# A recurrent attention step: the second V cast placed ahead of the second half's exponentials, and the second half's memory-query sums placed behind all of V's matmul groups

## Chip, cores and metric

The kernel runs on one core of a Trainium2 chip. The metric is the device time of one execution in microseconds (us). The kernel before takes 770.77 us, the median of three runs (770.53 to 771.61).

## What is computed

The output mixes two branches with a gate per token: `g * a + (1 - g) * b`. Branch `b` is a layer norm followed by a two-layer MLP with a gelu. Branch `a` is what most of the time goes to: attention over 64 segments of 32 tokens, in order, because each segment takes eight memory rows from the one before it.

```python
mem = mem0
for s in range(n_seg):                       # 64 segments, strictly one after another
    xs = x[:, s * seg_len:(s + 1) * seg_len, :]
    h = jnp.concatenate([mem, xs], axis=1)   # 8 memory rows + 32 tokens
    q, k, v = (einsum('btd,dhe->bhte', h, W) for W in (Wq, Wk, Wv))   # 32 heads of 128
    scores = where(mask, q @ k^T * scale, -1e9)
    p = softmax(scores)
    o = einsum('bhqk,bhke->bhqe', p, v)
    o = einsum('bhte,hed->btd', o, Wo)
    mem = o[:, :M, :]                        # rows of the 8 memory queries: the next segment's memory
    outs.append(o[:, M:, :])
return concatenate(outs, axis=1)
```

## The kernel before

A first stage computes the MLP branch and loads the attention weights. Then a loop of 64 steps (line 678 and on), one per segment, does the attention. Everything in a step hangs on the memory rows that the step before delivered, so the steps can't overlap, except for work that doesn't need the memory: the last eight tokens of each segment are projected for four segments at a time, and these "fill" units are handed out by `run(n)` at places in the step where TensorE would wait. The order of instructions on each engine is written out by hand (a manual schedule); each engine works through its own list in that order, and semaphores make it wait for others. The code's order is therefore the whole schedule.

What a step does, in the order of TensorE (PE in the profile), with the lines that the prediction uses:

1. Four projections for Q and K, sixteen matmuls each (`qk_unit`, L122), each cast by ScalarE (ACT, L127) and transposed by VectorE (DVE, L131).
2. `scores(s, 0)`: scores of heads 0 to 15 into PSUM bank `SbF` (L259, L263), then ScalarE's exponential over them into `E` (L713).
3. V of heads 0 to 15 into bank `X1`: four groups of four matmuls (`v_unit`, L141), one group for each 128 rows of the contraction (`kc`). The four matmuls of a group stand in four column strips of the array. Then the first group of V for heads 16 to 31 into bank `X2`.
4. `xsums(E, 0)` (L616) and `msum(0)` (L270, L273): small matmuls with a matrix of ones that add up the exponentials, of the token queries and of the memory queries. `mnorm(0)` on VectorE takes the reciprocal of the memory queries' sums (L709) and multiplies them onto their exponentials (L710).
5. `scores(s, 1)`: scores of heads 16 to 31 into bank `W`. On ScalarE: `exps(1, 0)` for the memory queries (64 columns, L702), the second cast of V's first half, `v_cast(0, 1)` (L719), and `exps(1, 1)` for the token queries (160 columns, L702).
6. Two more groups of V into `X2` (`kc` 1 and 2), then `msum(1)` with `mnorm(1)`, then V's last group (`kc` 3). ScalarE casts `X2` in two halves, `v_cast(1, 0)` and `v_cast(1, 1)` (L719).
7. Two fill units, `xsums(E, 1)` (L616), and `av`: exponentials times V into the four banks `U`, first heads 0 to 15 (sixteen L283, four L288), then heads 16 to 31 (the same again). The second sixteen need the product of `mnorm(1)` and the casts of `X2`: the first eight of them `v_cast(1, 0)`, the last eight `v_cast(1, 1)`.
8. ScalarE copies the memory queries' part out of `U` (L746), TensorE projects with Wo (L153), and eight small matmuls and three casts (L659, L661) turn the result into the next step's memory rows.

`mnorm(1)` is more tied up than it looks: its reciprocal reads the sums in `U[1]`, and writes into a spare part of bank `W`, the bank from which `exps(1, 1)` reads its scores. So it waits for `msum(1)` on TensorE and for `exps(1, 1)` on ScalarE, whichever is later.

The last step (s = 63) has no `msum` and no `mnorm`, and ends in a tail of its own.

Of the kernel before, what the change touches and what calls it, by code (L numbers as in the profile page):

```python
# [27 lines left out]
def kernel(ctx, tc, A_x, A_mem0, A_Wq, A_Wk, A_Wv, A_Wo, A_seg_len, B_x, B_w1, B_b1, B_w2, B_b2, gate_w, out):  # L28
# [9 lines left out]
    KC = Dm // P  # L38
# [55 lines left out]
    def load_xT(T):  # L94
        xT = ew.tile([P, KC, P], BF16, tag="xT", bufs=3, name="xT")
        nc.sync.dma_start_transpose(out=xT[:], in_=x2[T * P:(T + 1) * P, :])
        xTs[T] = xT
# [9 lines left out]
    X2 = lps.tile([P, 512], FP32)  # L107
# [11 lines left out]
    def qk_unit(bk, G, t, hf, kc):  # L119
        h0, h1 = HF[hf]  # L120
        for j in range(4):
            nc.tensor.matmul(bk[32 * j:32 * j + 32, :], lhsT=G[:, kc, :], rhs=W5[t][:, kc, h0:h1, j, :],  # L122
                             start=(kc == 0), stop=(kc == KC - 1), tile_position=(0, 32 * j))

    def qk_cast(bk):
        Tb = ew.tile([P, 8, 32, 2], BF16, tag="Tb", bufs=3, name="Tb")
        nc.scalar.copy(out=Tb[:], in_=bk.rearrange("p (a b e) -> p a e b", a=8, b=2))  # L127
        return Tb

    def qk_tr(Tb, dst, hf, c0=0):  # L130
        nc.vector.transpose(out=dst[:, 8 * hf:8 * hf + 8, c0:c0 + 32, :].rearrange("p a r b -> p a (r b)").bitcast(FP32),  # L131
                            in_=Tb[:].rearrange("p a e b -> p (a e b)").bitcast(FP32))
# [6 lines left out]
    def v_unit(bk, G, vb, kc):  # L139
        for j in range(4):  # L140
            nc.tensor.matmul(bk[32 * j:32 * j + 32, :], lhsT=G[:, kc, :], rhs=Wv5[:, kc, 4 * vb:4 * vb + 4, j, :],  # L141
                             start=(kc == 0), stop=(kc == KC - 1), tile_position=(0, 32 * j))
# [18 lines left out]
    def flush(q, n=1):  # L161
        for _ in range(min(n, len(q))):
            q.pop(0)()
# [17 lines left out]
    def vp_load(T, si):  # L181
        nc.sync.dma_start(VP[T % 2][:, si].rearrange("p v e -> p (v e)"), VLs[T][si:P:SPT].rearrange("p a v e -> p a (v e)"))
# [20 lines left out]
    def c_load(T):  # L203
        c = cw.tile([P, Dm], BF16, tag="c", name="c")
        nc.sync.dma_start(c[:], c_dr[T * P:(T + 1) * P, :])
        cs[T] = c
# [30 lines left out]
    def prep_h(s):  # L237
        T, si = divmod(s, SPT)
        nc.gpsimd.tensor_copy(out=hT[s % 3][:, :, 0:RIDE], in_=xTs[T][:, :, seg * si:seg * si + RIDE])
# [14 lines left out]
    def scores(s, i2):  # L254
        T, si = divmod(s, SPT)
        for i in range(4 * i2, 4 * i2 + 4):
            for j in range(4):
                h = 4 * i + j
                nc.tensor.matmul(Sb[i2][32 * j:32 * j + 32, i - 4 * i2, M:M + 40], lhsT=KT[:, h // 2, :, h % 2], rhs=QT[:, h // 2, :, h % 2],  # L259
                                 start=False, stop=True, skip_group_check=True, tile_position=(0, 32 * j))  # L260
        for j in range(4):
            a0 = 8 * i2 + j // 2
            nc.tensor.matmul(Sb[i2][32 * j:32 * j + 32].rearrange("p i (a b) -> p i a b", b=8)[:, :, 0:7:6, :],  # L263
                             lhsT=KL[T % 2][:, si, j // 2, i2].rearrange("p l a b -> p (l a) b")[:, :, j % 2],
                             rhs=QT[:, a0:a0 + 7:2, :, j % 2].rearrange("p a (x q) -> p a x q", q=8)[:, :, 0:5:4, :],
                             start=False, stop=True, skip_group_check=True, tile_position=(0, 32 * j))
# [323 lines left out]
    def side(T, si):  # L590
        gens = []
        if si == 2:
            if T >= 1:
                gens.append(wo_left(T - 1, X1))
        elif T + 1 < NT:
            gens = [[left_qk(T + 1, 0, 0, X1), left_qk(T + 1, 1, 0, X2)], [left_qk(T + 1, 0, 1, X1), left_qk(T + 1, 1, 1, X2)], [],
                    [left_v(T + 1, 0, X1), left_v(T + 1, 1, X2)]][si]
        return chain(*gens)
# [39 lines left out]
    def x_norm(s):  # L638
        T, si = divmod(s, SPT)
        XR, Rb = XRs.pop(s), Rbs.pop(s)[:].rearrange("p (c q) (h j) -> p h j c q", c=4, h=2)  # L640
        for out, o, a, b in ((UT[(s + 1) % 2], M, LEFT, 32), (UL[T % 2], LEFT * si, 0, LEFT)):
            for h in range(2):
                nc.gpsimd.tensor_tensor(out=out[:, :, 4 * h:4 * h + 4, o:o + b - a], in0=XR[:, :, 4 * h:4 * h + 4, a:b], in1=Rb[:, h, :, :, a:b], op=ALU.mult)  # L643
# [21 lines left out]
    for s in range(nseg):  # L665
        T, si = divmod(s, SPT)
        last = s == nseg - 1
        hc, hn = hT[s % 3], hT[(s + 1) % 3]
        W1, W2, W3 = WS[si]
        fill = side(T, si)  # L670
        if s + 1 < nseg:
            prep_h(s + 1)
        if s >= 1:
            x_norm(s - 1)
        if si == 0 and T >= 2:
            c_load(T - 2)
        if si < 3:
            vp_load(T, si + 1)
        if last:
            c_load(T - 1)  # L680
            c_load(T)
        if si == 0 and T + 2 < NT:
            load_xT(T + 2)
        for n, (t, hf) in enumerate(((0, 0), (1, 0), (0, 1), (1, 1))):
            bk = U[n]
            for kc in range(KC):
                qk_unit(bk, hc, t, hf, kc)
            if n == 0:
                flush(act_q, 9)
                flush(dve_q, 9)  # L690
            qk_tr(qk_cast(bk[:]), (QT, KT)[t], hf, LEFT * (1 - t))
            if n == 0:
                mask_put(1)
        V = cw.tile([P, NG, Dh], BF16, tag="V", name="V")
        E = cw.tile([P, NG, EW], BF16, tag="E", name="E")
        R = cw.tile([P, NG * 40], FP32, tag="R", name="R")
        Rs[s] = R
        xsum = SbF[:, 0:32 * NG].rearrange("p (i q) -> p i q", q=32)

        def exps(i2, x):  # L700
            c = slice(0, 40) if x else slice(40, EW)
            nc.scalar.activation(out=E[:, 4 * i2:4 * i2 + 4, c], in_=Sb[i2][:, :, c], func=ACTF.Exp, scale=scale)  # L702

        def msum(i2):
            sums(U[i2][:, 320:352].rearrange("p (i q) -> p i q", q=8), E[:, 4 * i2:4 * i2 + 4, :], 40, 48, 8, True)

        def mnorm(i2):
            r, e = RP[i2], E[:, 4 * i2:4 * i2 + 4, 40:56].rearrange("p i (a q) -> p i a q", q=8)
            nc.vector.reciprocal(out=r, in_=U[i2][:, 320:352])  # L709
            nc.vector.tensor_tensor(out=e, in0=e, in1=r.rearrange("p (i q) -> p i q", q=8).unsqueeze(2).to_broadcast([P, 4, 2, 8]), op=ALU.mult)  # L710

        scores(s, 0)
        nc.scalar.activation(out=E[:, 0:4, :], in_=Sb[0], func=ACTF.Exp, scale=scale)  # L713
        for kc in range(KC):
            v_unit(X1, hc, 0, kc)

        def v_cast(vb, h):
            i0 = 4 * vb + 2 * h
            nc.scalar.copy(out=V[:, i0:i0 + 2, :].rearrange("p i e -> p (i e)"), in_=(X1, X2)[vb][:, 256 * h:256 * h + 256])  # L719

        v_cast(0, 0)
        v_unit(X2, hc, 1, 0)
        if not last:
            xsums(E, 0)
            msum(0)
            mnorm(0)
        scores(s, 1)
        exps(1, 0)
        v_cast(0, 1)
        exps(1, 1)  # L730
        for kc in range(1, KC - 1):
            v_unit(X2, hc, 1, kc)
        if not last:
            msum(1)
            mnorm(1)
        v_unit(X2, hc, 1, KC - 1)
        for h in range(2):
            v_cast(1, h)
        if last:
            break  # L740
        run(W1)
        xsums(E, 1)
        recip_x(s)
        av(s, V, E)
        for j in (0, 2, 1, 3):
            nc.scalar.copy(out=UT[s % 2][:, j, :, 0:M], in_=U[j][:, 0:NG * 40].rearrange("p (i q) -> p i q", q=40)[:, :, 32:40])  # L746
        x_raw(s)
        run(W2)
        prep_q(s + 1)
        w = wo_pass(UT[s % 2], (0, P, 2 * P, Dm))  # L750
        if s >= 1:
            ws[s - 1] = w
        run(W3)
        for _ in extra(T, si):
            pass
        new_mem(w, hn, 0)
        run(1)
        new_mem(w, hn, 1)
        run(1)
        new_mem(w, hn, 2)  # L760
        for _ in fill:
            pass
        if si == 3 and T + 2 < NT:
            left_x(T + 2)
        flush(dve_q, 9)
        nc.vector.tensor_tensor(out=rmin[:, 0:RW], in0=rmin[:, 0:RW], in1=R[:, 0:RW], op=ALU.min)
        flush(act_q, 9)
# [174 lines left out]
```

## Time and profile before

| | |
|---|---|
| median of the runs | 770.77 us (770.53 to 771.61) |
| the profiled execution's own time: its span, first to last instruction | 768.4 us |
| what the median has beyond that span | 2.4 us |
| mean granted TensorE clock | 0.996 of full speed |
| busy: PE, ACT, DVE, POOL | 753.4, 540.0, 396.1, 278.2 us |
| bytes moved by DMA | 70.58 MB, 92 GB/s on average |

A row of the timeline gives the start in us, the duration in us, the engine, the line, the operation, what it writes and reads, the shape, and how many such instructions in a row were put together (x8). A duration of a merged row runs from the first start to the last end. PE is matmuls, PEld the loading of their stationary operand, which runs beside PE. In brackets stands how long the engine had been idle and what let it go on.

Busy time of PE has to be read with care: a matmul's row covers its way through the array, some 0.17 us for the smallest, and the next ones start long before it ends. A PE that waits 0.1 us for a semaphore still looks nearly busy. Waits are better read from the starts of two neighbouring rows.

### The profile page before, as it was taken

What the parts mean: (1) busy time and instruction counts of PE and PEld (TensorE: products, weight loads), DVE (VectorE), ACT (ScalarE), POOL (GpSimd) and SP (SyncE); (2) the same over time, 40 slices, a digit from 0 to 9 for tenths busy, and PEclk for the clock granted to TensorE, in tenths of its full rate; (3) what the DMA queues carried; (4) which work ended last, traced back from release to release, by engine and by line L of the source; (5) the groups of instructions that cost most, each with busy time, mean ns of one, the idle gap of its engine ahead of it and who ended that gap; (6) DMA issues with size and microseconds to landing.
All of it is one profiled execution on the core that took longest, in us unless ns stands there. A gap on an engine that the chain in (4) does not pass through costs nothing.

```text
span 768.4 us, 43822 instructions
## 1 busy us (share of the span) xinstructions
PE 753.4 (98%) x19186; PEld 412.2 (54%) x19186; DVE 396.1 (52%) x1428; ACT 540.0 (70%) x1631; POOL 278.2 (36%) x522
## 2 busy tenths in 40 slices
PE   7999999999999999999999999999999999999996
PEld 5666554555555555555555555555555555555553
DVE  5776355445445454545554554545454555444444
ACT  4666676777777777777777777777777777777763
POOL 4111033433344443334434334443424443343341
PEclk9999999999999999999999999999999999999999
DMA  6779422223222222212131322122222213122221
GB/s 196 274 233 400 153 58 63 76 63 87 65 59 66 79 72 73 80 53 74 58 89 62 90 63 79 45 80 73 80 72 59 76 49 89 62 83 64 72 67 38
DMA packets 53319, 70.58 MB, mean 92 GB/s; under 512 B 21306, under 2 KB 43043, under 8 KB 51587
## 3 DMA queue, kind: packets, MB, share of 16 engines
q1 hardware_dynamic: 51394, 64.84, 26.8%
q8 instruction: 152, 2.49, 1.4%
q0 software_dynamic: 784, 1.97, 0.8%
q10 hardware_dynamic: 944, 0.92, 0.3%
q14 instruction: 45, 0.36, 0.2%
HBM read 56.96 MB, written 4.45 MB: 80 GB/s over the span
## 4 chain that ended last, share of the span: by engine, by line
PE 96%; DMA 1%; DVE 1%; ACT 1%; issue 0%; SPq 0%; POOL 0%; DVEq 0%; ACTq 0%
PE U L122 30%; PE X L141 18%; PE W L153 15%; PE X L122 7%; PE U L468 4%; PE U L283 4%; PE X L153 4%; PE W L462 2%; PE SbF L462 2%; PE U L270 1%; PE W L259 1%; DMA w_sb<-in_B_w_dram 1%; PE U L659 1%; PE SbF L259 1%; PE SbF L616 1%; PE U L288 1%
## 5 line engine op out<-in xcount | busy, mean ns | idle before, releaser
L643 POOL TENSOR_TENSOR UT<-XR,Rb 128x384 bf16<-128x384 bf16 x126 | 140.3, 1136 | 301.7 <-DMA Rb<-r_dr 220.5
L127 ACT CAST Tb<-U 128x512 bf16<-128x512 f32 x258 | 151.2, 586 | 78.4 <-PE U L122 78.1
L122 PEld LDWEIGHTS <-hT 128*32 128x32 bf16 x4096 | 104.5, 96 | 103.9 <-DVE hT L661 8.6
L141 PE MATMUL X<-Wv_sb,hT 128*32 128x512 bf16 x2048 | 143.8, 378 | 0.0
L122 PE MATMUL U<-Wq_sb,hT 128*32 128x512 bf16 x2048 | 136.1, 381 | 0.3 <-DVE hT L661 0.2
L122 PE MATMUL U<-Wk_sb,hT 128*32 128x512 bf16 x2048 | 132.7, 379 | 0.0
L153 PE MATMUL W<-Wo_sb,UT 128*32 128x512 bf16 x2080 | 124.6, 380 | 1.2 <-POOL racc L635 1.2
L661 DVE CAST hT<-U 128x8 bf16<-128x8 f32 x126 | 20.9, 167 | 172.8 <-PE U L659 163.6
L719 ACT CAST V<-X 128x256 bf16<-128x256 f32 x256 | 88.7, 372 | 14.5 <-PE X L141 0.8
L131 DVE STREAM_TRANSPOSE QT<-Tb 128x256 f32<-128x256 f32 x128 | 57.0, 446 | 76.5 <-ACT Tb L127 76.5
L153 PEld LDWEIGHTS <-UT 128*32 128x32 bf16 x2080 | 57.8, 96 | 56.5 <-issue 13.1
L650 ACT CAST w<-W 128x128 bf16<-128x128 f32 (+1 forms) x192 | 46.0, 311 | 48.2 <-PE W L153 48.2
L622 ACT CAST XR<-U 128x256 bf16<-128x256 f32 x252 | 78.4, 434 | 0.0
L131 DVE STREAM_TRANSPOSE KT<-Tb 128x256 f32<-128x256 f32 x128 | 57.0, 445 | 28.0 <-ACT Tb L127 23.5
L643 POOL TENSOR_TENSOR UL<-XR,Rb 128x128 bf16<-128x128 bf16 x126 | 60.3, 502 | 0.0
L141 PEld LDWEIGHTS <-hT 128*32 128x32 bf16 x2048 | 46.4, 94 | 21.0
L635 POOL TENSOR_TENSOR racc<-racc,R 128x72 f32<-128x72 f32 x63 | 21.3, 338 | 93.4 <-PE U L288 84.1
L468 PE MATMUL U<-w_sb,hTm 128*128 128x512 bf16 (+1 forms) x176 | 52.4, 381 | 0.0
L746 ACT CAST UT<-U 128x64 bf16<-128x64 f32 x252 | 35.4, 226 | 22.9 <-PE U L288 22.8
L462 PEld LDWEIGHTS <-w_sb 128*128 128x128 bf16 (+1 forms) x352 | 34.5, 102 | 20.1 <-issue 1.3
L702 ACT ACTIVATE E<-W 128x64 bf16<-128x64 f32 (+1 forms) x128 | 35.0, 273 | 11.3 <-PE W L263 11.3
L659 PEld LDWEIGHTS <-w 128*32 128x32 bf16 x1008 | 22.8, 93 | 37.2 <-ACT w L650 29.3
(159 smaller groups left out, 1204.7 us busy)
## 6 DMA issues: line engine op xcount, KB each, us to landing
Rb<-r_dr SPq DMA_DIRECT2D x63, 512.0 KB, 3.8
Wv_sb<-in_A_Wv_dram SPq DMA_DIRECT2D x4, 1024.0 KB, 6.3
Wq_sb<-in_A_Wq_dram SPq DMA_DIRECT2D x4, 1024.0 KB, 7.1
Wk_sb<-in_A_Wk_dram SPq DMA_DIRECT2D x4, 1024.0 KB, 9.4
Wo_sb<-in_A_Wo_dram SPq DMA_DIRECT2D x4, 1024.0 KB, 15.0
VP<-VL SPq DMA_DIRECT2D x64, 64.0 KB, 3.5
c<-c_dr SPq DMA_DIRECT2D x16, 128.0 KB, 3.6
xt<-in_A_x_dram SPq DMA_DIRECT2D x15, 128.0 KB, 3.1
```

Of the source, the lines that this page charges most:

```text
L122: nc.tensor.matmul(bk[32 * j:32 * j + 32, :], lhsT=G[:, kc, :], rhs=W5[t][:, kc, h0:h1, j, :], start=(kc == 0), stop=(kc == KC - 1), tile_ ...
L127: nc.scalar.copy(out=Tb[:], in_=bk.rearrange("p (a b e) -> p a e b", a=8, b=2))
L131: nc.vector.transpose(out=dst[:, 8 * hf:8 * hf + 8, c0:c0 + 32, :].rearrange("p a r b -> p a (r b)").bitcast(FP32), in_=Tb[:].rearrange("p ...
L141: nc.tensor.matmul(bk[32 * j:32 * j + 32, :], lhsT=G[:, kc, :], rhs=Wv5[:, kc, 4 * vb:4 * vb + 4, j, :], start=(kc == 0), stop=(kc == KC - ...
L153: nc.tensor.matmul(bk[32 * c:32 * c + 32, :], lhsT=U_[:, j, i, :], rhs=Wo_sb[:, 4 * i + j, :], start=(n == 0), stop=(n == NW - 1), tile_po ...
L462: nc.tensor.matmul(hp[:rows, 0:TB * P], lhsT=w1_sb[:, kc, fc * P:fc * P + rows], rhs=yTs[blk][:, kc, :], start=(kc == 0), stop=(kc == KC - 1))
L468: nc.tensor.matmul(bp(blk, tt)[:], lhsT=hTm[blk % 2][:rows, fc, tt * P:(tt + 1) * P], rhs=w2_sb[:rows, fc, :], start=(fc == 0), stop=(fc = ...
L622: nc.scalar.copy(out=XR[:, j], in_=U[j][:, 0:NG * 40].rearrange("p (i q) -> p i q", q=40)[:, :, 0:32])
L643: nc.gpsimd.tensor_tensor(out=out[:, :, 4 * h:4 * h + 4, o:o + b - a], in0=XR[:, :, 4 * h:4 * h + 4, a:b], in1=Rb[:, h, :, :, a:b], op=ALU ...
L650: nc.scalar.copy(out=w[:, a:b], in_=W[:, a:b])
L719: nc.scalar.copy(out=V[:, i0:i0 + 2, :].rearrange("p i e -> p (i e)"), in_=(X1, X2)[vb][:, 256 * h:256 * h + 256])
L746: nc.scalar.copy(out=UT[s % 2][:, j, :, 0:M], in_=U[j][:, 0:NG * 40].rearrange("p (i q) -> p i q", q=40)[:, :, 32:40])
```

## The change

`v_cast(0, 1)` goes ahead of both exponentials of the second half on ScalarE. On TensorE all three remaining groups of V go ahead of `msum(1)`. The instructions are the same ones, with the same shapes; VectorE, GpSimd and the DMA queues keep their order.

```diff
         scores(s, 1)
+        v_cast(0, 1)
         exps(1, 0)
-        v_cast(0, 1)
         exps(1, 1)
-        for kc in range(1, KC - 1):
+        for kc in range(1, KC):
             v_unit(X2, hc, 1, kc)
         if not last:
             msum(1)
             mnorm(1)
-        v_unit(X2, hc, 1, KC - 1)
         for h in range(2):
             v_cast(1, h)
```

## The prediction, made before the change was run

> **What bounds the kernel now.** I read the page first, then the list of waits, then the timeline of single steps. The page and the chain that ended last say that TensorE carries everything:
>
> ```profile
> span 768.4 us, 43822 instructions
> PE 753.4 (98%) x19186; PEld 412.2 (54%) x19186; DVE 396.1 (52%) x1428; ACT 540.0 (70%) x1631; POOL 278.2 (36%) x522
> PE 96%; DMA 1%; DVE 1%; ACT 1%; issue 0%; SPq 0%; POOL 0%; DVEq 0%; ACTq 0%
> ```
>
> So the order on ACT and PE matters only where PE stands still. The list of waits (engine, line, what released it: us in total, times, longest) shows whether it does at the edited place:
>
> ```profile
> DVE SbF L709 <- ACT V L719: 21.1, 63, 0.3
> ACT E L702 <- PE W L263: 11.3, 64, 0.5
> PEld L270 <- issue: 15.6, 65, 0.5
> DVE W L709 <- ACT E L702: 12.0, 48, 0.6
> DVE W L709 <- PE X L141: 3.9, 14, 0.5
> ```
>
> The third row is the weight loads of the memory-query sums: 65 waits, 0.24 us each on average, about one per step. The fourth and fifth say that the second reciprocal waits in every step too. The steps resemble each other, so I work in one, the step at 317 us; all that is worked out below is within it and taken 63 times (steps 0 to 62; the last one is treated apart).
>
> ```profile
> 315.14 1.04 PE L122 MATMUL U<-Wq_sb,hT 128*32 128x512 bf16 x16
> ...
> 316.00 1.04 PE L122 MATMUL U<-Wk_sb,hT 128*32 128x512 bf16 x16
> ...
> 318.08 0.37 ACT L719 CAST V<-X 128x256 bf16<-128x256 f32 x1
> ...
> 318.16 0.19 PE L273 MATMUL U<-E,BO 128*32 128x32 bf16 x4
> ...
> 318.33 0.15 PEld L141 LDWEIGHTS <-hT 128*32 128x32 bf16 x8
> 318.35 0.61 PE L141 MATMUL X<-Wv_sb,hT 128*32 128x512 bf16 x8
> 318.49 0.37 DVE L709 RECIPROCAL SbF<-U 128x32 f32<-128x32 f32 x1 [0.33 <-ACT V L719]
> 318.57 0.10 PEld L270 LDWEIGHTS <-BO 128*32 128x32 bf16 x1
> 318.63 0.23 ACT L702 ACTIVATE E<-W 128x64 bf16<-128x64 f32 x1 [0.17 <-PE W L263]
> 318.75 0.37 ACT L719 CAST V<-X 128x256 bf16<-128x256 f32 x1
> ...
> 318.90 0.20 PE L270 MATMUL U<-E,BO 128*32 128x32 bf16 x4
> ...
> 318.93 0.20 PE L273 MATMUL U<-E,BO 128*32 128x32 bf16 x4
> ...
> 318.95 0.40 PE L141 MATMUL X<-Wv_sb,hT 128*32 128x512 bf16 x4
> ...
> 319.00 0.32 ACT L702 ACTIVATE E<-W 128x160 bf16<-128x160 f32 x1
> 319.17 0.62 PE L122 MATMUL X<-Wq_sb,GL 128*32 128x512 bf16 x8
> 319.35 0.37 DVE L709 RECIPROCAL W<-U 128x32 f32<-128x32 f32 x1 [0.24 <-ACT E L702]
> ...
> 319.40 0.65 ACT L719 CAST V<-X 128x256 bf16<-128x256 f32 x2
> 319.60 0.22 PE L616 MATMUL SbF<-BO,E 128*32 128x4 bf16 x8
> ...
> 319.75 0.29 PE L283 MATMUL U<-E,V 32*128 32x40 bf16 x16
> 319.75 0.22 DVE L710 TENSOR_TENSOR E<-E,W 128x64 bf16<-128x64 bf16 x1
> ...
> 319.87 0.21 PE L288 MATMUL U<-E,VP 32*128 32x64 bf16 x4
> ...
> 320.03 0.30 PE L283 MATMUL U<-E,V 32*128 32x40 bf16 x16
> ...
> 320.17 0.19 PE L288 MATMUL U<-E,VP 32*128 32x64 bf16 x4
> ```
>
> Two stalls of PE are to be seen. A group of four 512-column matmuls takes 0.215 us of PE (two neighbouring projections, four groups each, start 316.00 - 315.14 = 0.86 apart). Two V groups from 318.35 are through at 318.78, yet the sums start at 318.90: **stall one, 0.12 us**, until the memory exponential (318.63 + 0.23 = 318.86) is in. The second stall: the first sixteen L283 start at 319.75, their four L288 at 319.87, and the second sixteen only at 320.03, which is 0.06 behind the end of `mnorm(1)`'s product (319.75 + 0.22 = 319.97). So **stall two, some 0.13 us, belongs to mnorm(1)**, and its chain is exps(1, 1), over at 319.32, reciprocal at 319.35, product, second half of `av`. That chain ends last; stall one stands in front of work that waits again.
>
> **The change, part by part.** No instruction is added or taken away; what counts is where each one starts.
>
> *ACT.* Two casts in a row start 0.65 - 0.37 = 0.28 apart, so `v_cast(0, 1)` starts at 318.08 + 0.28 = 318.36, in time in which ACT sat idle for the scores. From a cast to the exponential behind it the starts are 319.00 - 318.75 = 0.25 apart: `exps(1, 0)` could start at 318.61, and the scores let it go at 318.63. The cast costs nothing, by a margin of 0.02; if it were late, the memory exponential would still have the 0.14 us that its reader gives it below. `exps(1, 1)` follows 318.75 - 318.63 = 0.12 behind, at 318.75, and ends at 319.07 instead of 319.32: **0.25 earlier**.
>
> *PE.* Three V groups from 318.35 are through at 318.35 + 3 x 0.215 = 319.00. The exponential has been there since 318.86, so stall one is gone. `msum(1)` starts at 319.00 and its L273 at 319.02 or 319.03 (0.03 behind, as in 318.90 to 318.93). The fill starts at 319.05 instead of 319.17, and all up to the first half of `av` comes 0.12 earlier.
>
> *mnorm(1)*, which ends last. Its reciprocal waits for two. exps(1, 1) would let it go at 319.10 (319.07, and 0.03 as between 319.32 and 319.35). For the other, the sums, PE's way to DVE has to be priced. The first reciprocal waits for `msum(0)`: L273 at 318.16, L709 at 318.49, 0.33 later. (The list names ACT's cast as its releaser; by the code it doesn't read that cast.) A second price, of smaller matmuls:
>
> ```profile
> 323.18 0.19 PE L659 MATMUL U<-SelM,w 128*32 128x8 bf16 x4
> ...
> 323.49 0.43 DVE L661 CAST hT<-U 128x8 bf16<-128x8 f32 x2 [2.72 <-PE U L659]
> ```
>
> That is 0.31. I take 0.33, the same operation with the same shape. The second reciprocal then starts at 319.02 + 0.33 = **319.35, exactly where it starts now.** The 0.25 that ACT gives is worth nothing, because the sums have moved 0.09 back and now end last. The product ends at 319.97 and the second half of `av` starts at 320.03, as before. PE's 0.12 are not lost on the way; they are given back in front of `av`. By the 0.31 it would be 0.02 earlier; by the rounding of starts and the spread of the four L273 it could be 0.01 later. Bounds -0.02 to +0.01; I take +0.003, as 3 x 0.215 and 0.03 add up to a little over 319.02.
>
> *The casts of X2.* V is complete 0.17 earlier: its last group starts at 318.35 + 0.43 = 318.78 instead of 318.95. The casts start 0.45 behind it (318.95 to 319.40), so at 319.23, with ACT free by then, and end at 319.88 instead of 320.05. Now 320.05 is 0.02 behind the start of the second sixteen L283, whose last eight need it. From the first L283 to the first L288 it takes 319.87 - 319.75 = 0.12 in the first half and 320.17 - 320.03 = 0.14 in the second. The first half has a small hold of its own (its second matmul writes the bank that the reciprocal reads until 319.72), so the cast holds the second half by 0.02, bounds 0.00 and 0.03. **That hold goes.** It is the one thing on the path that gets shorter, and the copies L746 and all behind them follow `av`.
>
> *Other queues.* No DMA moves. VectorE and GpSimd keep their order, and their work before the reciprocal is over by then (product of `mnorm(0)`: 318.49 + 0.37 + 0.22 = 319.08). In the last step ACT's part is alone:
>
> ```profile
> 754.41 0.65 ACT L719 CAST V<-X 128x256 bf16<-128x256 f32 x2
> 754.51 0.29 PE L270 MATMUL SbF<-E,BO 128*32 128x256 bf16 x4
> ...
> 755.11 0.83 PE L153 MATMUL X<-Wo_sb,UL 128*32 128x512 bf16 x12
> ```
>
> The sums at 754.51 wait for exps(1, 1) and could come 0.25 earlier, but L153 behind them writes X2, whose cast ends at 755.06 now and then. I take 0; it gains at most 0.25.
>
> *Sum.* 63 x (-0.020 + 0.003) = -1.1 us. Made against the span of 768.4 it gives 767.3. The median of the runs lies 2.4 above the profiled span, and nothing edited lies outside the span: 770.77 - 1.1 = **769.7 us**, or 0.14% less.
>
> A rule that speaks against the change: the Trainium skill, page "TensorE: Matmul & The Clock Gate", Part 3, "The mechanism", says that a weight load overlaps matmuls in flight only where its row group differs. V's groups and the sums use all rows. By that rule the sums' loads couldn't hide behind V's last group, and it is the second rival below. The trace speaks against it: the load of BO at 318.57 runs for 0.10 while the eight V matmuls of 318.35 are in flight to 318.96.
>
> **The rivals.**
>
> 1. *Stall one pays in full.* Then the second half of `av` would also come 0.12 earlier: 63 x 0.12 = 7.6, so 763.2. For it: 65 waits of PE at that place. Against it: the 0.06 between the product and the second half. It needs a reciprocal at 319.23, 0.20 behind L273, and neither price (0.33, 0.31) is near that.
> 2. *The sums come later than I reckon* (the other side). With V's last group ahead of them, the four loads of BO at 0.10 run only when that group is through: `msum(1)` starts at 319.10, the reciprocal at 319.45, the second half of `av` at 320.13. Less the 0.02 of the cast, 63 x 0.08 = 5.0 slower: 775.8. It decides from L273 at 319.045, 0.02 behind my figure; from 319.07 it is over 0.2%. For it: no row shows these sums right behind a V group without a wait. Against it: the load at 318.57.
> 3. *The sums' release is quicker,* 0.31 or a little under: reciprocal at 319.33 or 319.32, 63 x (0.02 + 0.02 to 0.03) = 2.5 to 3.2 faster, 768.3 to 767.6. For it: the L661 row. Against it: L273 itself at 0.33.
> 4. *The cast holds nothing:* 0 to +0.6 us, 770.8 to 771.4, within 0.2%.
>
> **How the numbers follow.** A measurement of this kernel tells about 0.2% from no change, which is 1.5 us. Forecast (769.1 to 770.5): 0.48. Rival 4: 0.14. Rival 3: 0.15. Rival 1: 0.06. Rival 2, with every lateness of that kind beyond 319.07: 0.17, its start nearer to 772 than 775.8. Faster by over 0.2%: rivals 1 and 3, 0.21. Slower by over 0.2%: rival 2, 0.17. Within 0.2%: the forecast and rival 4, 0.62. The range 768.2 to 772.0 takes in the forecast, rival 4, two thirds of rival 3 and the start of rival 2 (0.07): 0.79.
>
> **What would show it.** L270's wait for issue falls from 15.6 us to under 2. ACT's wait at L702 for the scores goes. The second reciprocal names PE's L273 as releaser in all but a few steps, and starts 1.00 behind the V groups' first start as now (319.35 - 318.35). The X2 casts start 0.88 behind it instead of 1.05, and PE's pause before the second sixteen L283 grows by 0.1 or is split with one before the second L283. What would prove me wrong: the reciprocal moved by over 0.02 either way, or L270 more than 0.65 behind the V groups' start.

## The result, and the profile after

The changed kernel takes 772.65 us, the median of 12 runs (771.2 to 774.61); the kernel before took 771.07 in 12 runs on the same chip (769.07 to 772.89). The ratio is 1.0022, with a 95% interval of 1.0012 to 1.0031: slower by 0.9 to 2.4 us. I had forecast 769.7, a gain of 1.1, and a range that ended at 772.0.

The page of the kernel after, its span, its busy times and the shares of the chain that ended last:

```profile
span 770.2 us, 43822 instructions
PE 754.3 (98%) x19186; PEld 419.4 (54%) x19186; DVE 392.1 (51%) x1428; ACT 533.6 (69%) x1631; POOL 277.8 (36%) x522
...
PE 96%; DVE 1%; DMA 1%; ACT 1%; issue 0%; POOL 0%; DVEq 0%; ACTq 0%; POOLq 0%
```

The same number of instructions, and nothing that stands out: the mean clock granted to TensorE was 0.999, against 0.996 before. The list of waits (what waited, what released it: us in total, times, longest) shows that the edit did what it says:

```profile
DVE SbF L709 <- PE U L273: 21.1, 63, 0.3
DVE W L709 <- PE U L273: 18.1, 61, 1.0
...
DVE W L709 <- PE SbF L616: 1.3, 2, 0.6
...
ACT E L702 <- PE W L263: 0.6, 1, 0.6
```

L270's 65 waits for issue (15.6 us) are down to one of 0.2 us, and ACT's 11.3 us at L702 to 0.6. The second reciprocal (`W L709`) waited for ACT's exponential in 48 steps; now it waits for the sums in 61. One step of the timeline, to be laid beside the step at 317 us in the prediction:

```profile
318.98 0.65 ACT L719 CAST V<-X 128x256 bf16<-128x256 f32 x2
...
319.05 0.19 PE L273 MATMUL U<-E,BO 128*32 128x32 bf16 x4
...
319.25 0.82 PE L141 MATMUL X<-Wv_sb,hT 128*32 128x512 bf16 x12
...
319.39 0.37 DVE L709 RECIPROCAL SbF<-U 128x32 f32<-128x32 f32 x1 [0.34 <-PE U L273]
...
319.69 0.22 PEld L270 LDWEIGHTS <-BO 128*32 128x32 bf16 x4
...
319.90 0.19 PE L270 MATMUL U<-E,BO 128*32 128x32 bf16 x4
...
319.93 0.19 PE L273 MATMUL U<-E,BO 128*32 128x32 bf16 x4
...
320.12 0.65 ACT L719 CAST V<-X 128x256 bf16<-128x256 f32 x2 [0.17 <-PE U L273]
...
320.29 0.37 DVE L709 RECIPROCAL W<-U 128x32 f32<-128x32 f32 x1 [0.28 <-PE U L273]
...
320.52 0.46 PE L283 MATMUL U<-E,V 32*128 32x40 bf16 x16
...
320.69 0.22 DVE L710 TENSOR_TENSOR E<-E,W 128x64 bf16<-128x64 bf16 x1
...
320.96 0.28 PE L283 MATMUL U<-E,V 32*128 32x40 bf16 x16
321.07 0.21 PE L288 MATMUL U<-E,VP 32*128 32x64 bf16 x4
321.32 0.56 ACT L745 CAST UT<-U 128x64 bf16<-128x64 f32 x4 [0.55 <-PE U L288]
```

Counted from the V groups' first start, 319.25, the sums' first row L270 stands at +0.65, the reciprocal at +1.04 and the second sixteen L283 at +1.71. In the step of before they stood at 0.55, 1.00 and 1.68. PE's pause has moved into `av`: the first sixteen L283 now spread over 0.46 (0.29 before), since their second matmul writes the bank that the reciprocal reads until 320.66.

Single rows are rounded to 0.01 us, and what matters here is of that size. So I took medians over the trace's steps. The table gives them for the 47 of the 63 looped steps in which s is not a multiple of four, in us behind the V groups' first start; the columns right of "after" are experiments, told below.

| | before | after | e1_act | e2_pe | e4_before_r0 | e6_after_const | e9_act_31 |
|---|---|---|---|---|---|---|---|
| sums, first L273 | 0.573 | 0.673 | 0.582 | 0.674 | 0.573 | 0.674 | 0.583 |
| second reciprocal | 1.000 | 1.032 | 0.907 | 1.033 | none | none | 0.908 |
| product, end | 1.622 | 1.654 | 1.528 | 1.654 | 1.119 | 1.218 | 1.528 |
| X2 casts, end | 1.691 | 1.516 | 1.700 | 1.518 | 1.691 | 1.517 | 1.702 |
| second sixteen L283 | 1.675 | 1.707 | 1.581 | 1.706 | 1.537 | 1.414 | 1.590 |
| last eight L283 | 1.747 | 1.762 | 1.756 | 1.761 | 1.747 | 1.573 | 1.655 |
| copies of `U` (L746) | 2.038 | 2.063 | 2.048 | 2.062 | 2.039 | 1.865 | 2.017 |
| whole step | 10.230 | 10.257 | 10.240 | 10.254 | 10.233 | 10.056 | 10.207 |

The reciprocal comes 0.032 later, and so do the product and the second sixteen; the copies come 0.025 later, and what hangs on them too: the step is longer by 0.027. In the 16 steps with s a multiple of four Wo's pass starts 0.018 later. 47 x 0.027 + 16 x 0.018 = 1.6 us, which is what the runs show (772.65 - 771.07). The loop of the profiled execution is longer by 2.8 us. The other 1.2 come from single irregular steps: of those 16, six (s = 8, 16, 24, 28, 40 and 44) are longer than in before by 0.10 to 0.40, and the other ten by 0.01 to 0.03. One execution of each kernel doesn't show whether such steps belong to the change. That the typical steps add up to the runs' 1.6 to the tenth is therefore in part luck; more on irregular steps stands at the end.

### The profile page after: what moved, and what is told of

The parts are those of the page before. It is cut to its first block, busy times and chain, and to the rows that moved or that the text cites. A ratio compares the mean times of both kernels' runs of the same rounds, so it can differ in the third digit from the quotient of the medians.

```text
span 770.2 us, 43822 instructions
## 1 busy us (share of the span) xinstructions
PE 754.3 (98%) x19186; PEld 419.4 (54%) x19186; DVE 392.1 (51%) x1428; ACT 533.6 (69%) x1631; POOL 277.8 (36%) x522
## 4 chain that ended last, share of the span: by engine, by line
PE 96%; DVE 1%; DMA 1%; ACT 1%; issue 0%; POOL 0%; DVEq 0%; ACTq 0%; POOLq 0%
PE U L122 29%; PE X L141 18%; PE W L153 15%; PE X L122 8%; PE U L283 5%; PE U L468 5%; PE X L153 4%; PE SbF L462 2%; PE W L462 2%; PE W L259 1%; PE U L659 1%; PE SbF L259 1%; DMA b1r<-in_B_b_dram 1%; PE SbF L616 1%; PE U L288 1%; PE U L273 0%
## 5 line engine op out<-in xcount | busy, mean ns | idle before, releaser
L122 PEld LDWEIGHTS <-hT 128*32 128x32 bf16 x4096 | 104.3, 96 | 104.0 <-DVE hT L661 9.0
L122 PE MATMUL U<-Wq_sb,hT 128*32 128x512 bf16 x2048 | 136.1, 381 | 0.3 <-DVE hT L661 0.2
L141 PE MATMUL X<-Wv_sb,hT 128*32 128x512 bf16 x2048 | 133.2, 378 | 0.0
L122 PE MATMUL U<-Wk_sb,hT 128*32 128x512 bf16 x2048 | 132.6, 379 | 0.0
L153 PE MATMUL W<-Wo_sb,UT 128*32 128x512 bf16 x2080 | 124.6, 380 | 1.2 <-POOL racc L635 1.2
L719 ACT CAST V<-X 128x256 bf16<-128x256 f32 x256 | 82.7, 375 | 20.8 <-PE U L273 11.2
L153 PEld LDWEIGHTS <-UT 128*32 128x32 bf16 x2080 | 57.3, 96 | 57.7 <-issue 14.8
L283 PE MATMUL U<-E,V 32*128 32x40 bf16 x2048 | 45.8, 178 | 1.8 <-DVE W L709 1.6
```

What stands on the lines that cost most here:

```text
L153: nc.tensor.matmul(bk[32 * c:32 * c + 32, :], lhsT=U_[:, j, i, :], rhs=Wo_sb[:, 4 * i + j, :], start=(n == 0), stop=(n == NW - 1), tile_po ...
L283: nc.tensor.matmul(Uv[j][:, i, :], lhsT=V[q, i, :], rhs=E[q, i, 8:48], start=(i == 0), stop=False, skip_group_check=True, tile_position=(3 ...
```

## The experiments

My theory after this trace: the change brings forward all that stands around the second reciprocal, and that reciprocal alone takes it back, because PE's way to DVE takes longer when the sums follow a 512-column group without a pause. Its rivals: ACT's part costs something by itself; the sums themselves come too late; the X2 cast, not the reciprocal, sets the end. Each run is compared with the kernel before on the same chip, whose median stands in brackets.

**e1_act: ACT's part alone.**

```diff
-        exps(1, 0)
         v_cast(0, 1)
+        exps(1, 0)
         exps(1, 1)
```

> ACT's part of the change alone: v_cast(0, 1) ahead of both exponentials, msum(1) between V's groups as before. Theory 1 (the sums moved behind V release the second reciprocal later, and that is the whole loss): no loss here. The sums start 0.55 us after V's first group as before, the reciprocal is let go by them at about 0.90 instead of 1.00, but the last eight matmuls of av then wait for the second X2 cast (over at 1.69 as before), so the step hardly gets shorter: ratio to before 0.999 to 1.000. Theory 2 (the cast in front of the exponentials is what costs): as slow as the changed kernel, ratio 1.002. Theory 3 (the typical step is not longer, irregular steps are): ratio anywhere within 0.998 to 1.002, with the typical step of 10.23 us unchanged.

Measured: 771.08 us (771.24), ratio 1.0000, 0.9992 to 1.0009. Its timeline:

```profile
319.19 0.61 PE L141 MATMUL X<-Wv_sb,hT 128*32 128x512 bf16 x8
...
319.78 0.20 PE L273 MATMUL U<-E,BO 128*32 128x32 bf16 x4
...
320.10 0.37 DVE L709 RECIPROCAL W<-U 128x32 f32<-128x32 f32 x1 [0.15 <-PE U L273]
...
320.25 0.65 ACT L719 CAST V<-X 128x256 bf16<-128x256 f32 x2 [0.35 <-PE X L141]
...
320.50 0.22 DVE L710 TENSOR_TENSOR E<-E,W 128x64 bf16<-128x64 bf16 x1
...
320.78 0.40 PE L283 MATMUL U<-E,V 32*128 32x40 bf16 x16
321.02 0.20 PE L288 MATMUL U<-E,VP 32*128 32x64 bf16 x4
321.24 0.56 ACT L746 CAST UT<-U 128x64 bf16<-128x64 f32 x4 [0.35 <-PE U L288]
```

Reciprocal and product come 0.09 earlier than before, the second sixteen L283 too, and nothing is gained: their last eight wait for the cast (over at 320.90), so the sixteen spread over 0.40, and the copies start 0.34 behind the cast's end. The same 0.34 to 0.35 stands in the kernel before, whose cast ended at 320.05:

```profile
320.39 0.56 ACT L746 CAST UT<-U 128x64 bf16<-128x64 f32 x4 [0.35 <-PE U L288]
```

So before, two chains ended within 0.01 us of each other. The product gives copies at its end plus 0.409 (after: 1.654 to 2.063), which for before is 2.031; the cast gives its end plus 0.347, which is 2.038. ACT's part frees the first and leaves the second. It even pushes that one by 0.009: the memory exponential starts when it did and ends 0.008 later (0.505 against 0.497), and L273 and V's last group follow.

**e2_pe: TensorE's part alone**, all three V groups ahead of the sums, ACT in its old order.

```diff
-        for kc in range(1, KC - 1):
+        for kc in range(1, KC):
             v_unit(X2, hc, 1, kc)
         ...
-        v_unit(X2, hc, 1, KC - 1)
```

> TensorE's part alone: msum(1) behind all V groups, ScalarE's order as before. Theory 1: the same reciprocal as in the changed kernel, 1.03 us after V's first group, since exps(1, 1) lets it go at 1.00 and the sums at 1.03; typical step 10.257 instead of 10.230 us, ratio 1.002. Theory 2: as before, ratio 1.000. Theory 3: typical step 10.23.

Measured: 771.96 us (771.24), ratio 1.0008, 0.9999 to 1.0016.

```profile
320.20 0.82 PE L141 MATMUL X<-Wv_sb,hT 128*32 128x512 bf16 x12
...
320.88 0.19 PE L273 MATMUL U<-E,BO 128*32 128x32 bf16 x4
...
321.24 0.36 DVE L709 RECIPROCAL W<-U 128x32 f32<-128x32 f32 x1 [0.28 <-ACT E L702]
```

The row names ACT as the releaser, but exps(1, 1) is over at 0.968 in the median and let the reciprocal go at 1.000 in the kernel before; here it starts at 1.033, 0.359 behind L273, to the nanosecond as in the kernel after. So the lengthening in the trace is TensorE's part, whatever ACT's order. The timing is weaker: 0.7 us, with an interval that takes in zero; the 1.4 of the trace's steps (47 x 0.024 + 16 x 0.015) lies just beyond its upper end of 1.2.

**e3_swap: the kernel after with exps(1, 1) ahead of exps(1, 0)**, so that the sums stand behind all V groups and PE pauses ahead of them all the same.

```diff
         v_cast(0, 1)
-        exps(1, 0)
         exps(1, 1)
+        exps(1, 0)
```

> The changed kernel with its two exponentials swapped, so that the one that the sums need comes last and TensorE stands still before them again. It tests the size of the step from the sums to the second reciprocal, which was 0.36 us from the first L273 in the changed kernel (right behind V's last group, no pause) and 0.33 with ScalarE's part alone (TensorE had waited). Theory 1 (the release takes longer when the sums stand right behind a 512-column group): 0.33 here, though the order of TensorE is that of the changed kernel; the sums start about 0.80 us after V's first group. Rival (it is the place behind all V groups, or the fill behind the sums, that makes it longer): 0.36 again. The kernel is slower either way, by the 0.11 to 0.15 us per step by which the reciprocal is later, 7 to 9 us.

Measured in a single execution, so without an interval: 775.72 us (769.84), span 773.9, typical step 10.324, which is 0.067 above after. I had expected a step longer by 0.11 to 0.15, with the sums at 0.80; they came at 0.754, the exponential being quicker in than I reckoned.

```profile
322.39 0.20 PE L270 MATMUL U<-E,BO 128*32 128x32 bf16 x4
...
322.41 0.20 PE L273 MATMUL U<-E,BO 128*32 128x32 bf16 x4
...
322.74 0.37 DVE L709 RECIPROCAL W<-U 128x32 f32<-128x32 f32 x1 [0.35 <-PE U L273]
```

The reciprocal, the second sixteen and the copies are later than after by 0.072, 0.070 and 0.070: the reciprocal sets the end there. And it starts 0.324 behind L273, as in e1_act, where PE pauses too, and not 0.359. The place in the order is that of the kernel after; only the pause came back, and the way to DVE got shorter by 0.035.

**e4_before_r0 and e5_after_r0: no second reciprocal**, in before and in after. The second half's memory exponentials are multiplied by the first half's reciprocals, so these outputs are other numbers. The copy of the two reciprocals into `R` (L633) then takes the first half's twice, in e6_after_const too; those lines are not shown below.

```diff
+            if i2 == 0:
-            nc.vector.reciprocal(out=r, in_=U[i2][:, 320:352])
+                nc.vector.reciprocal(out=r, in_=U[i2][:, 320:352])
-            nc.vector.tensor_tensor(out=e, in0=e, in1=r...
+            nc.vector.tensor_tensor(out=e, in0=e, in1=RP[0]...
```

> The kernel before without the second reciprocal: the second half's memory exponentials are multiplied with the first half's reciprocals (so the second half's sums are computed and not used). Theory 1: the product no longer ends last, but the second X2 cast does, over at 1.69 us after V's first group, with the last eight matmuls of av 0.05 behind it; so almost nothing is won: ratio to before 0.998 to 1.000. Rival (the second reciprocal's hold is the only one at that place): 0.15 us per step, ratio 0.988.

Measured: 771.02 us (771.24), ratio 1.0003, 0.9992 to 1.0015. The timeline of e4_before_r0:

```profile
320.00 0.65 ACT L720 CAST V<-X 128x256 bf16<-128x256 f32 x2
...
320.50 0.43 PE L283 MATMUL U<-E,V 32*128 32x40 bf16 x16
...
321.00 0.56 ACT L747 CAST UT<-U 128x64 bf16<-128x64 f32 x4 [0.35 <-PE U L288]
```

The product ends half a microsecond earlier and the copies start where they did, 0.35 behind the cast's end at 320.65. In the kernel before the cast by itself is enough to hold the whole step at its length.

> The same with the change in it: no second reciprocal, the first half's reciprocals in its place. Theory 1 (the change does bring sums, fill and X2 casts forward, and only the second reciprocal takes it back): the last eight matmuls of av start about 1.57 us after V's first group instead of 1.75 to 1.76, some 0.17 to 0.20 us per step, 10 to 12 us in all, ratio to before 0.985 to 0.987. Rival (something else of the change costs: PE order, ACT order): ratio 1.000 or above, or no better than the kernel before without the second reciprocal.

Measured: 769.58 us (771.24), ratio 0.9975, 0.9963 to 0.9988. That is far from the 0.985 to 0.987 expected, and the miss is of my making: the product now reads `RP[0]`, which lies in bank `SbF`, and `xsums(1)` writes that bank, so PE waits for it at a new place, in every step:

```profile
PEld L616 <- issue: 19.3, 63, 0.5
```

`xsums(1)` starts at 1.308 instead of 1.129, 0.05 behind the product's end at 1.255, and `av` behind it. The run doesn't settle the question.

**e6_after_const: the same without that tie.** The kernel after; the second half's memory exponentials are multiplied by the constant 0.025 and not by reciprocals of their sums.

```diff
+            if i2 == 1:
+                nc.vector.tensor_scalar(out=e, in0=e, scalar1=0.025, scalar2=None, op0=ALU.mult)
+                return
```

> The changed kernel without the second reciprocal, the second half's memory exponentials multiplied by a constant (1/40) in place of their own reciprocals. In the run with the first half's reciprocals that product read bank SbF, and xsums(1), which writes it, waited for the product (1.31 us after V's first group instead of 1.13); a constant takes that wait away. Theory 1: xsums(1) at 1.13, the second sixteen L283 no later than 1.45, their last eight 0.05 behind the X2 cast at 1.57; 0.17 to 0.20 us per step less than the changed kernel and before, ratio to before 0.983 to 0.987. Rival (something else of the change costs): ratio 0.995 or above.

Measured: 761.32 us (769.84), ratio 0.9884, 0.9870 to 0.9898.

```profile
316.26 0.83 PE L141 MATMUL X<-Wv_sb,hT 128*32 128x512 bf16 x12
...
316.93 0.19 PE L273 MATMUL U<-E,BO 128*32 128x32 bf16 x4
...
317.13 0.65 ACT L722 CAST V<-X 128x256 bf16<-128x256 f32 x2 [0.17 <-PE U L273]
...
317.30 0.18 DVE L710 TENSOR_SCALAR E<-E 128x64 bf16<-128x64 bf16 x1 [0.28 <-PE U L273]
...
317.53 0.27 PE L283 MATMUL U<-E,V 32*128 32x40 bf16 x16
...
317.68 0.38 PE L283 MATMUL U<-E,V 32*128 32x40 bf16 x16
...
318.12 0.56 ACT L748 CAST UT<-U 128x64 bf16<-128x64 f32 x4 [0.35 <-PE U L288]
```

With the reciprocal's 0.4 out of the chain the step is 10.056, shorter than before by 0.174, and the cast, 0.174 earlier, sets the end again (317.78 to 318.12). Here is the gain that the change makes ready, 8.5 us by the medians (10.9 by its typical steps, 47 x 0.174 + 16 x 0.172, the latter from the start of Wo's pass; irregular steps take some of it back), and e4_before_r0 shows that the old order couldn't take it. One instruction chain, sums to reciprocal to product, stands between.

**e7_halves and e8_last_half: the same end by TensorE.** If cast and reciprocal each set the end when the other is freed, V's half for the first cast has to be complete ahead of the sums, and its other half behind them. Both stand on e1_act. e7_halves cuts the V groups kc 1 to 3 of X2 into halves of 256 columns (12 more matmuls and 12 more loads a step); e8_last_half cuts only the last group (4 more of each). The cut of e7_halves, against e1_act, without the helper `v_half` and the stop flags:

```diff
-        for kc in range(1, KC - 1):
-            v_unit(X2, hc, 1, kc)
+        for kc, h in ((1, 0), (2, 0), (3, 0), (1, 1), (2, 1)):
+            v_half(X2, hc, 1, kc, h)
         if not last:
             msum(1)
             mnorm(1)
-        v_unit(X2, hc, 1, KC - 1)
+        v_half(X2, hc, 1, 3, 1)
```

> An attempt to beat both: ScalarE's part of the change, and V's remaining groups for X2 as 256-column halves, the first half's three ahead of the second half's, the sums ahead of the very last. So the sums keep their early place (0.55 us after V's first group) and the X2 casts, which ended last in the kernel before, start at about 0.65 and 0.95 instead of 1.04 and 1.31. Theory 1 (two chains end within 0.01 us of each other before av's end, product and X2 cast, and only lifting both pays): second sixteen L283 at 1.58 instead of 1.67, with no hold of the last eight, 0.08 to 0.11 us per step, 5 to 7 us in all, ratio to before 0.991 to 0.994. Rival (256-column groups cost TensorE more than half a 512-column group, because of twelve more weight loads): the gain shrinks by 6 times what a group takes beyond 0.108 us; at 0.125 us each there is none.

Measured: 772.87 us (769.84), ratio 1.0044, 1.0027 to 1.0062: slower. Yet the typical step is 10.135, shorter by 0.095 as expected (47 x 0.095 + 16 x 0.095 = 6.0 us), with the second sixteen L283 at 1.582 and the copies at 1.942. The time goes in irregular steps. The 63 steps of before are 2.5 us longer in all than the medians of their kinds (by s modulo 4), and 12 of them are over by more than 0.06; those of e7_halves are 12.6 us longer, 28 of them by more than 0.06. (Its profiled execution took 774.77 us, 1.9 above the median of its runs.) The waits of e7_halves (its L158 is L153 of before, its L288 the L283):

```profile
PEld L158 <- issue: 16.3, 44, 1.0
...
PEld L288 <- issue: 5.1, 12, 0.7
```

In before, L153 waits 13.2 us for issue, 0.3 at the longest, and L283 1.5 us. Waits of up to 1.0 us at these lines, for which the profile shows no releaser, are new. But they don't need more instructions: e6_after_const, which has no more than before, waits up to 1.2 us for issue at L122.

> ScalarE's part of the change, and of V's groups only the last one cut in two halves of 256 columns, one ahead of the sums and one behind them: eight instructions of TensorE more per step than before instead of twenty-four. Theory 1 (two chains end side by side, and lifting both pays): the same typical step as with all three groups cut, 10.14 us instead of 10.23 (sums at 0.56, V complete and X2 casts at about 0.95, second sixteen L283 at 1.58). Theory on the irregular steps (there the run with all groups cut lost its gain: 28 steps with 12.6 us in excess; TensorE's instructions come in too slowly when it has more of them in less time): an excess of 3 to 7 us, so 3 to 0 us faster than before, ratio 0.995 to 1.001; if the excess has nothing to do with the number of instructions, 12 us again and ratio 1.004.

```diff
+        v_half(X2, hc, 1, KC - 1, 0)
         if not last:
             msum(1)
             mnorm(1)
-        v_unit(X2, hc, 1, KC - 1)
+        v_half(X2, hc, 1, KC - 1, 1)
```

Measured: 771.28 us (770.9), ratio 1.0006, 0.9993 to 1.0019. The best steps are again 10.133 to 10.137, but those with s = 3 modulo 4 take 10.197. Of the 16 with s a multiple of four nine are shorter than in before (their median over all 16: 10.475, before 10.565), and seven take 10.79 or more (before: four). In all the steps are 9.0 us longer than their medians, 24 of them by more than 0.06, which is above the 3 to 7 that I had expected. The same two rows of e8_last_half:

```profile
PEld L158 <- issue: 16.6, 48, 1.0
...
PEld L288 <- issue: 4.3, 12, 0.8
```

**e9_act_31: the same end by ACT.** On e1_act, the two casts of X2 are cut 384 to 128 columns and no longer 256 to 256. Then only four of the second sixteen L283 wait for the second cast, and no longer eight. No instruction is added.

```diff
-            i0 = 4 * vb + 2 * h
-            nc.scalar.copy(out=V[:, i0:i0 + 2, :]..., in_=(X1, X2)[vb][:, 256 * h:256 * h + 256])
+            a, b = ((0, 2), (2, 4))[h] if vb == 0 else ((0, 3), (3, 4))[h]
+            nc.scalar.copy(out=V[:, 4 * vb + a:4 * vb + b, :]..., in_=(X1, X2)[vb][:, Dh * a:Dh * b])
```

> ScalarE's part of the change, and the two X2 casts cut 384 and 128 columns instead of 256 and 256, no instruction more than before. Theory 1 (with ScalarE's part alone the second X2 cast ends last, product and first X2 cast are 0.1 us earlier): now only the last four L283 wait for it, at about 1.75 us after V's first group, where the last eight waited at 1.756; what stands behind them is 0.02 to 0.03 shorter: typical step 10.21 to 10.22 us instead of 10.24, ratio to before 0.998 to 0.999. Rival (the second cast holds av at its start, not by its end): step 10.24, ratio 1.000.

Measured: 769.78 us (770.9), ratio 0.9983, 0.9971 to 0.9995: faster than both kernels, if by little.

```profile
319.01 0.61 PE L141 MATMUL X<-Wv_sb,hT 128*32 128x512 bf16 x8
...
320.06 0.65 ACT L719 CAST V<-X 128x384 bf16<-128x384 f32 x2 [0.35 <-PE X L141]
...
320.60 0.37 PE L283 MATMUL U<-E,V 32*128 32x40 bf16 x16
320.80 0.19 PE L288 MATMUL U<-E,VP 32*128 32x64 bf16 x4
321.02 0.56 ACT L746 CAST UT<-U 128x64 bf16<-128x64 f32 x4 [0.31 <-PE U L288]
```

The casts end at 320.71, as late as in e1_act, but fewer matmuls wait for that end, and the copies start 0.31 behind it instead of 0.34. Step 10.207, 0.023 under before: 47 x 0.023 + 16 x 0.015 = 1.3 us, against 1.1 in the medians.

## Why the prediction was wrong

- **Stall one goes and its 0.12 is given back in front of `av`.** Right. L270 at +0.65 as reckoned (3 x 0.215), L273 at 0.673, where I had 0.67 to 0.68; `xsums(1)` at 1.129 instead of 1.245; the pause that took it back stands between the first and the second L283 (0.024 apart before, 0.182 now), while that ahead of the second sixteen stayed at 0.15.
- **The sums take ACT's place as the reciprocal's last wait.** Right, in 61 of 63 steps.
- **"I take 0.33, the same operation with the same shape"** is the step that failed. The mechanism held and this term was mis-sized: behind V's last group PE's way to DVE, from the first L273, took 0.359. The reciprocal moved by +0.032 and not by +0.003, beyond my bound of +0.01 and beyond the 0.02 that I had named as what would prove me wrong. Shape and operation were the same; what stood ahead of them was not. e3_swap, the same order with a pause, gives 0.324; e2_pe, the other ACT order without one, 0.359. The rows that I priced by had small matmuls ahead (`msum(0)`: 0.333) and I didn't look for that.
- **The hold of the X2 cast, -0.02 per step.** The hold is real and it went: the last eight L283 stood 0.056 behind the cast's end in before, in e4_before_r0 and in e6_after_const, and by themselves would have stood 0.055 behind the second sixteen (after: 1.707 to 1.762), at 1.730 instead of 1.747. But to the copies it was worth 2.038 - 2.031 = 0.007. I took the delay of a matmul for a delay of what waits for its result: where the last eight L283 run through, the way from the last L288 to the copies is longer by 0.011 (0.229 against 0.218), the same effect as at the reciprocal, and takes most of the gain back.
- **Sum.** Per step +0.032 - 0.007 = +0.025 in place of -0.017; 63 x 0.025 = 1.6 us in place of -1.1.
- **"The cast costs nothing, by a margin of 0.02."** Nearly. The exponential behind it ends 0.008 later. In after a margin hides that; in e1_act it is the 0.010 by which the step grew.
- **Rival 2 had the side and not the mechanism.** It let the sums start late, behind loads that can't hide. The loads of `BO` ran at 319.69 for 0.22, while the twelve V matmuls of 319.25 were in flight to 320.07, and L270 started 0.65 behind the groups, with nothing added. This answers the rule that the Trainium skill gives on the page "TensorE: Matmul & The Clock Gate", Part 3, "The mechanism", by which a load overlaps matmuls in flight only where its row group differs: both use all rows here, and the trace doesn't agree. It fits what that page of the Trainium skill allows in Part 2, "Step-by-step: what each phase is for": a load pulled ahead into a background weight buffer. Whether that buffer was used no run shows. No rival of mine had the sums on time and their release late.
- **Rivals 1, 3 and 4.** Stall one didn't pay (772.65, not 763.2); the release was not quicker; the cast held next to nothing, as rival 4 had it, but the reciprocal's delay came on top.
- **What the change's ingredients are worth is shown by both neighbours**: take the reciprocal out and the changed order is faster by 1.2% (e6_after_const); leave the order of the sums alone and nothing is lost (e1_act).

## What to carry to other kernels

Where two chains end within a hundredth of a microsecond of each other, freeing one gains nothing: work out the end that each chain gives by itself, at the first instruction that waits for both, before a stall is priced. A release from TensorE is priced by a row with the same work *ahead* of the matmul, not only with the same matmul; an edit that closes a pause can lengthen the release of what follows it, here by 0.035 us. And where the trace's typical step gets shorter and the time doesn't, count the irregular steps.

## What the runs showed of the hardware

- From the last of the four L273 to the reciprocal on VectorE it took 0.301 us where TensorE had paused ahead of the sums (e1_act, e3_swap), 0.321 behind the small matmuls of `xsums` (`msum(0)`), 0.345 directly behind a 512-column group (after, e2_pe). ScalarE's copies behind the last L288 show the same in small: 0.217 or 0.218 where the cast had held the last eight L283 (before, e1_act, e4_before_r0, e6_after_const), 0.229 or 0.230 where they ran through (after, e2_pe, e3_swap), and 0.246 in e5_after_r0, where neither half of `av` had waited. Matmul starts in the trace thus say less about when a result is there, the denser TensorE is filled. The rows of the matmuls themselves don't show it: the four L273 last 0.19 us in after and 0.20 in e3_swap. That fits what the Trainium skill says on the page "Perfetto Trace Analysis", section "Tensor Engine Instruction (MATMUL, LD_WEIGHTS)": a matmul's shown start is that of reading its operands, and its shown end is estimated from its size and a delay for SBUF, so the wait for the array and the write to PSUM can't be seen. That the matmuls ahead drain meanwhile is my reading; no run isolates it.
- TensorE pauses at irregular places, and most in the kernels with more instructions. The steps lie 2.5 us in all beyond their medians in before, 9.0 with 8 more instructions a step (4 matmuls and 4 loads, e8_last_half), and 12.6 with 24 more (e7_halves). e6_after_const, with no more instructions in a shorter step, has 5.6, so a faster step alone may bring some; the other kernels lie between 1.6 and 4.6, which says how far a single execution can stray.
- The traces point to the supply of instructions, which I had named as a theory and didn't test by a run. TensorE's instructions come in packets of 16 KB: the queue `q8 instruction` has 152 of them in before and 158 in e7_halves, whose program has 1536 more instructions, so 256 instructions are a packet. Between 150 and 720 us two neighbouring starts on TensorE (matmuls and loads) lie more than 0.55 us apart nowhere in before, 4 times in e6_after_const, 8 times in e8_last_half and 14 times in e7_halves. Of these 26 pauses 25 end 1.2 to 1.6 us after a packet has landed, although packets land only every 4.4 us or so. Of the 13 in the other kernels 10 do. From one pause of e7_halves to the next, the recorded TensorE instructions number a multiple of 256, to within 8. No run changes the supply alone, so that it is the cause stays a reading of the traces.

The row of that queue on the page (packets, MB, share of the 16 DMA engines), in before and in e7_halves:

```profile
q8 instruction: 152, 2.49, 1.4%
...
q8 instruction: 158, 2.59, 1.4%
```
